# One table of moves in a convolution beside a gated unit: stores given to SyncE, late loads, fewer matmuls under the kernel's making, more in the spectra, output in halves

## The chip, the cores and the metric

The kernel runs on one core of one Trainium2 chip. The metric is the device time of one execution in microseconds (us). Before the change the median of 3 runs is 724.4 us (723.02 to 726.36). The profile comes from one further execution, whose own time is given below. TensorE (PE) multiplies matrices, VectorE (DVE) and ScalarE (ACT) work element by element, GpSimd (POOL) is a third and slower such engine, SyncE (SP) only issues transfers. ACT and POOL also issue transfers, in the one order in which all their instructions stand.

## The reference, cut to what matters

A row of the input is one of 2048 tokens with 448 channels; everything is float32.

```python
xn = _layernorm(x, axis=-1)
# A: a convolution over the tokens, its kernel K made from 256 complex modes per channel
P = jnp.exp((A * dt[:, None])[:, :, None] * pos[None, None, :])
K = 2.0 * jnp.einsum("dn,dnl->dl", C, P).real
y = jnp.fft.irfft(jnp.fft.rfft(u_t, L2) * jnp.fft.rfft(K, L2)[None], L2)[:, :, :L]
# B: a gated unit with 1792 inner columns
h = _sigmoid(xn @ w_gate) * (xn @ w_up)
out = x + (y + u * D_skip) + h @ w_down        # u_t is u = xn, tokens last
```

## The kernel before, in words

Two streams of work share the core, each written as a generator, and a planner takes turns between them. `conv` makes A, `glu` makes B and adds the residual x.

**conv.** First the modes are prepared. Then the convolution kernel K is made in 56 *chunks* of 8 channels (`kgen`). A chunk takes the angles' matmul (`tr`, L533) from a small tile `ph` that SP loads two pairs of chunks ahead (`phase_load`, L479 to 483), four ACT instructions for sines and cosines (`S`, L541 to 544), powers by POOL (`me`, `mf`, L511), three wide DVE products (`Et`, `Et`, `Ft`, L602 to 604), and 32 small matmuls (`ko`, L618; in the trace each is two, so 64). Every fourth chunk its result goes through a first stage of the transform (`kp`, `kq`, L559) and by ACT into DRAM (`sk_d`). Then comes `spectra`: 17 *steps*, one for each set of frequencies. A step loads the spectra's first stages of K (`skl`) and of the input (`sx`), transforms them (`there`, L891, 32 + 32 matmuls in the trace), multiplies them (DVE L897 to 905, POOL or DVE L907 and 908), makes halves (L912 and 913) and, two steps later, transforms them back (`back`, L926), writes them to DRAM (`v_d`) and reads them turned round (`vp`). `last` (L954 to 973) is the final transform from `vp`, once for each half h of the channels and each quarter q of the tokens: 32 matmuls in the trace, then DVE adds them to the accumulator. For h = 1 it then stores the rows of q to the output (L973).

**glu.** The tokens go in two halves of 1024, each as two tiles t of 512. For each of 14 pieces f of the inner columns and each t a `gate` does 11 matmuls for w_gate and 11 for w_up (`gu`, L709; "a gate half" below is 11 of them), then tanh by ACT (`th`, L717), a product by DVE (L720), and a split into high and low parts (`hh` by ACT, L725, `hl` by DVE, L727). After a group of 3 (once 2) pieces the down products run: per block b of 128 tokens 9 (or 6) matmuls (`po`, L812), which DVE adds to the accumulator `acc` (L817). The accumulators start as the residual x, loaded by `x_load` (L234). Half 0's are stored to `acc_d` (L832) and come back late in `spectra` as `ac`; half 1 takes the same two buffers, so its residual loads can start only when these stores have landed. These loads are issued by ACT.

**The crossing.** While the last group of half 0 runs, the second 1024 tokens come in, in four pairs (b = 8, 10, 12, 14): loaded, normalised, transposed (L207), and put through the first stage of the input's transform (`pair_first`, L685: 16 matmuls L273, four copies L693 by ACT into tiles `x1`, each stored by two transfers, L279, to `x1_d`; "x" and "x_d" in the trace). Two of the four copies go to a buffer that the next pair uses again (`wraw`), two to a pair of small buffers (`rd`).

**What sets the order.** The planner (L1135 to 1154) gives the next turn to the stream with the smaller share of its total done. A turn's share is the number that the generator yields: `WK / 3` three times a chunk, `WS / 2` twice a step, `2.5` a gate half, `0.6 * fc` a down block. The totals are in L1136. In `spectra` the turns simply alternate. `glu` stops after the first block of its last group (`yield None`, L803) and goes on when `conv` is written out; `last(1, q)` is written into its last blocks (L822 to 825). A scheduler then orders each engine's instructions by its own estimate of when each is ready; `tc.issue_after(x)` adds an order edge behind x for those instructions of the block that run on x's engine. Each engine runs its instructions strictly in the order that results.

```python
    total = [sum(Y0) + 11 * WP + 8 * WX + AHEAD + NCK * WK + HOLE + 19 * WS, 2 * (4 + NFT * 14.8) - HELD]
        i = min(live, key=lambda i: done[i] / total[i])
```

Of the kernel before, what the change touches and what calls it, by code (L numbers as in the profile page):

```python
# [20 lines left out]
D = 448  # L21
# [5 lines left out]
TWO_PI = 2.0 * math.pi  # L27
MAGIC = 1.5 * 2.0**23
NFT = F // 128
WK = 4.83  # L30
WS = 5
HOLE = 6
AHEAD = 34
WP = 5
WX = 2
HELD = 9
LASTS = 1
HP = 300
Y0 = (8, 1)
CP = D // 4  # L40
# [6 lines left out]
ORDER = [GROUPS, GROUPS[2:] + GROUPS[1::-1]]  # L47
# [79 lines left out]
def s4d_glu_kernel(ctx, tc, io):  # L127
    nc = tc.nc
# [556 lines left out]
    def pair_first(b, xns):  # L685

        x1 = pg.tile([128, 2, D], F32, name="x1", tag="wraw", bufs=1)
        pss = [psg.tile([128, 512], F32, name="gu", bufs=4) for _ in range(4)]
        for g in range(4):
            x_first_stage(pss[g][:, :D], xns, g)  # L690
        for g in range(4):
            to = x1[:, g] if g < 2 else pg.tile([128, D], F32, name="x1", tag="rd", bufs=RB)
            nc.scalar.copy(to, pss[g][:, :D])  # L693
            x1_store(row(b, g), to, nc.scalar)

    def gate(w, xs, to, between=None):
        wh, wl = w
# [32 lines left out]
    def glu():  # L730
        stores, later = [], []
        for half in range(2):
            if half == 1:
                for q in (2, 3):
                    accs.append(acc_tile())
                    x_load(accs[q], 4 * q, 4, [nc.scalar])
            for fs_ in ORDER[half]:
                fc, f0 = len(fs_), fs_[0]
                wts, ws, hs = [], [], [[], []]
# [12 lines left out]
                for n_, (f, t) in enumerate(order):  # L752
                    if t == 0:
                        wh = pg.tile([128, 2, 4, 128], F32R, name="wh", bufs=2)
                        if half == 0:
                            first = len(raws) == 2
                            raw, rd = raws.pop()
                            wl = w_low()
                            with hp(HP):
                                nc.scalar.copy(wh, raw)  # L760
                                if first:
                                    v.scalar_tensor_tensor(wl, raw, lim[:, 0, 0:1], wh, ALU.mult, ALU.subtract)
                                else:
                                    v.tensor_tensor(wl, raw, wh, ALU.subtract)
                            if not raws and f + 1 < NFT:
                                raws.append((w_load(f + 1), None))
                            stores.extend(kept((wh, wl), wt_d, f))
                        else:
                            wl = w_low()
                            for t_, d_ in kept((wh, wl), wt_d, f):  # L770
                                nc.sync.dma_start(t_, d_)
                        ws.append((wh, wl))
                    between = (lambda s_=mid[n_]: step(*s_)) if cross and mid[n_] else None
                    yield from gate(ws[f - f0], xq[2 * half + t], hs[t], between)
                    for t_, d_ in stores:
                        nc.sync.dma_start(d_, t_)
                    stores[:] = later
                    later.clear()
                    if t == 0:
                        dh = pg.tile([128, D], F32R, name="dh", bufs=FCH[0])  # L780
                        if half == 0:
                            rd = rd or rd_load(f)
                            dl = d_low()
                            with hp(HP), tc.issue_after((act if f == 1 else marks)[0].ins):
                                nc.scalar.copy(dh, rd)
                            nc.gpsimd.tensor_tensor(dl, rd, dh, ALU.subtract)
                            later.extend(kept((dh, dl), dt_d, f))
                        else:
                            dl = d_low()
                            for t_, d_ in kept((dh, dl), dt_d, f):  # L790
                                nc.sync.dma_start(t_, d_)
                        wts.append((dh, dl))
                    yield 2.5
                    for s_ in end[n_] if cross else ():
                        step(*s_)
                    if cross:
                        yield 2
                for t in range(2):
                    acc = accs[2 * half + t]
                    for b in range(4):  # L800
                        if final and (t, b) == (0, 1):

                            yield None  # L803
                        bs = slice(128 * b, 128 * b + 128)
                        end_ = final and (t, b) == (1, 3)
                        for h, ds in enumerate((slice(0, H), slice(H, D)) if end_ else (slice(0, D),)):
                            po = psg.tile([128, D], F32, name="po", tag="gu", bufs=4)
                            n = 0
                            with tc.issue_after(sp_mm[0].ins) if glu_on else nullcontext():
                                for (hh, hl), (dh, dl) in zip(hs[t], wts):  # L810
                                    for a_, w_ in ((hh, dh), (hh, dl), (hl, dh)):
                                        glu_mm[:] = [nc.tensor.matmul(  # L812
                                            po[:, ds], a_[:, bs], w_[:, ds], start=(n == 0), stop=(n == 3 * fc - 1)
                                        )]
                                        n += 1
                            with hp(HP):
                                v.scalar_tensor_tensor(  # L817
                                    acc[:, b, ds], po[:, ds], 0.5, acc[:, b, ds], ALU.mult, ALU.add
                                )
                            if final and t == 1 and b > 1:  # L820
                                out_end(acc[:, b : b + 1], 12 + b, ds)
                        if final and (t, b) == (1, LASTS):  # L822
                            sp_mm[:] = glu_mm
                            for q in range(4):
                                lasts[0](1, q)
                        if final and (t, b) == (1, 1):
                            out_end(acc[:, 0:2], 12, slice(0, D))
                        yield 0.6 * fc
                        if cross and (t, b) in downs:
                            step(*downs[t, b])  # L830
                    if cross:
                        nc.sync.dma_start(acc_d[:, 4 * t : 4 * t + 4], acc)  # L832

    def spectra(pf):
# [119 lines left out]
        def last(h, q):  # L954
# [15 lines left out]
                a = acc[:, p::2, ds]  # L970
                v.tensor_tensor(a, a, half(pb[q % 2][:, p, : 2 * H]), ALU.add)
            if h == 1 and q < 3:
                out_end(acc, 4 * q, slice(0, D), *([[nc.gpsimd]] if q == 0 else []))  # L973

        ac = acl[0]
        vts = [pf.tile([128, 4, H], F32, name="vt", bufs=2) for _ in range(2)]
# [57 lines left out]
        back(*made)  # L1034
        sp_mm[:] = glu_mm
        turned(*made[:2], 8, nc.gpsimd)
        back(*made_, (nc.sync, nc.scalar))
        turned(*made_[:2], 8)

# [141 lines left out]
```

## Time and profile before

| | |
|---|---|
| median of 3 runs | 724.4 us (723.02 to 726.36) |
| the profiled execution's own time | 727.67 us |
| its span, first to last instruction | 725.9 us |
| busy in the span: PE, DVE, ACT, POOL | 659.1, 575.6, 420.3, 351.6 us |
| first chunk's `ko` matmuls start, last chunk's | 146.2, 533.0 us |
| first step of `spectra`, last `back`'s first matmul | 547.7, 689.7 us |
| transfers | 125.76 MB, mean 173 GB/s |

In the answers below a row of the timeline reads: start in us, length in us, engine, line, operation, result<-operands, shapes, count, and in brackets the idle time of the engine before it and what ended that. A row of the chain of waits reads: start, length, what it was. A row of a table of stretches reads: from:to, length, then for PE, PEld (weight loads), DVE, ACT and POOL the busy us and (instructions), then the granted share of PE's clock, the mean busy share of the transfer engines, and GB/s. A matmul's row in a table of groups has the mean ns of one from issue to end; since matmuls overlap in the array, the time that a run of them takes is read from the chain.

### The profile page before, as it was taken

Reading aid. Unit: us, or ns where it says so; the run is one execution under the profiler, and the core shown is the slowest. Engines: PE = TensorE matmul, PEld = TensorE weight load, DVE = VectorE, ACT = ScalarE, POOL = GpSimd, SP = SyncE. Lnnn points to the kernel's source line nnn. Section 1 sums busy time; section 2 is a strip of 40 time slices with the busy share of each in tenths; the row PEclk is TensorE's granted clock in tenths of the full one; section 3 lists DMA queues with packets and bytes.
Section 4 is the critical chain, followed back from the end, with each engine's and each line's share of the span. In section 5 each row is a group of like instructions: output and inputs, shape, how many; then the busy total and the mean of one; then the engine's idle time right before and its main releaser. Section 6 shows DMA issues by size and latency. Waiting matters only on the chain.

```text
span 725.9 us, 20720 instructions
## 1 busy us (share of the span) xinstructions
PE 659.1 (91%) x8581; PEld 509.7 (70%) x8581; DVE 575.6 (79%) x779; ACT 420.3 (58%) x651; POOL 351.6 (48%) x395
## 2 busy tenths in 40 slices
PE   2798999999999899988979999999989999999784
PEld 1675788877778677655857887887776677777463
DVE  5689998699878798986548978897747989886823
ACT  3635455686678879996468768876822342332300
POOL 2111006785887879995335585686403224321101
PEclk9899999999899999999989999999989999999876
DMA  9977749645126454553962342433469787874456
GB/s 207 263 230 218 204 158 289 217 167 178 40 77 190 123 143 127 147 143 89 259 166 76 97 120 72 119 83 101 132 173 373 235 283 248 280 234 158 145 162 203
DMA packets 93630, 125.76 MB, mean 173 GB/s; under 512 B 12784, under 2 KB 79536, under 8 KB 93280
## 3 DMA queue, kind: packets, MB, share of 16 engines
q1 hardware_dynamic: 72000, 107.15, 46.9%
q10 hardware_dynamic: 20816, 14.91, 8.6%
q0 software_dynamic: 720, 2.36, 1.3%
q8 instruction: 68, 1.11, 0.6%
q14 instruction: 26, 0.21, 0.1%
HBM read 72.09 MB, written 52.30 MB: 171 GB/s over the span
## 4 chain that ended last, share of the span: by engine, by line
PE 49%; DVE 19%; DMA 10%; ACT 10%; issue 5%; POOL 3%; ACTq 1%; SPq 1%; DVEq 0%; POOLq 0%
PE gu L709 21%; PE po L812 13%; DVE Et L602 4%; DVE Ft L604 4%; DVE Et L603 3%; PE ko L618 3%; POOL me L511 2%; PE pk L891 2%; PE tr L533 2%; DMA x_d<-x 2%; PE px L891 2%; ACT S L544 2%; ACT S L541 2%; PE pk L926 1%; ACT S L542 1%
## 5 line engine op out<-in xcount | busy, mean ns | idle before, releaser
L511 POOL TENSOR_TENSOR me<-me,pm 128x32 f32<-128x32 f32 (+1 forms) x168 | 134.5, 801 | 97.3 <-DVE Et L603 85.1
L511 POOL TENSOR_TENSOR mf<-mf,pm 128x64 f32<-128x64 f32 (+1 forms) x112 | 121.0, 1080 | 5.8
L709 PE MATMUL gu<-xh,wh 128*128 128x512 f32 x336 | 103.5, 413 | 4.1 <-ACT xh L216 4.0
L603 DVE TENSOR_TENSOR Et<-me,S 128x1024 f32<-128x1024 f32 x56 | 79.2, 1414 | 23.0 <-ACT me L524 20.6
L709 PE MATMUL gu<-xh,wl 128*128 128x512 f32 x336 | 96.1, 392 | 0.0
L709 PE MATMUL gu<-xl,wh 128*128 128x512 f32 x336 | 95.9, 391 | 0.0
L812 PE MATMUL po<-dh,hh 128*128 128x448 f32 (+1 forms) x227 | 87.8, 387 | 2.9 <-DVE acc L817 1.4
L812 PE MATMUL po<-dh,hl 128*128 128x448 f32 (+1 forms) x227 | 84.9, 376 | 0.0
L725 ACT CAST hh<-gu 128x512 fp32r<-128x512 f32 x56 | 33.0, 590 | 89.3 <-DVE gu L720 82.5
L812 PE MATMUL po<-dl,hh 128*128 128x448 f32 (+1 forms) x227 | 84.6, 373 | 0.0
L604 DVE TENSOR_TENSOR Ft<-mf,S 128x1024 f32<-128x1024 f32 x56 | 78.3, 1399 | 7.5 <-POOL mf L511 3.9
L602 DVE TENSOR_TENSOR Et<-me,S 128x1024 f32<-128x1024 f32 x56 | 75.6, 1351 | 8.3 <-ACT S L544 7.9
L709 PEld LDWEIGHTS gu<-xh,wh 128*128 128x128 f32 x336 | 61.6, 193 | 26.6 <-issue 7.6
L618 PE MATMUL ko<-Et,Ft 128*32 128x64 f32 x3584 | 65.0, 224 | 12.4 <-DVE Ft L604 12.1
L618 PEld LDWEIGHTS ko<-Et,Ft 128*32 128x32 f32 x3584 | 54.8, 112 | 30.5 <-DVE Ft L604 16.8
L817 DVE SCALAR_TENSOR_TENSOR acc<-po,acc 128x448 f32<-128x448 f32 (+1 forms) x81 | 48.5, 609 | 33.0 <-PE po L812 33.0
L709 PEld LDWEIGHTS gu<-xh,wl 128*128 128x128 f32 x336 | 62.9, 188 | 14.6 <-DVE hl L727 0.7
L709 PEld LDWEIGHTS gu<-xl,wh 128*128 128x128 f32 x336 | 62.9, 188 | 14.2 <-issue 0.7
L541 ACT ACTIVATE S<-tr 128x1024 f32<-128x1024 f32 x56 | 57.9, 1034 | 25.7 <-PE tr L533 15.6
L907 POOL TENSOR_TENSOR yy<-yy 128x448 f32<-128x448 f32 (+1 forms) x16 | 23.5, 1471 | 92.7 <-DVE yy L904 92.7
L544 ACT ACTIVATE S<-S,hpi 128x1024 f32<-128x1024 f32 x56 | 65.9, 1176 | 0.1
L542 ACT ACTIVATE S<-tr 128x1024 f32<-128x1024 f32 x56 | 57.8, 1032 | 0.0
(204 smaller groups left out, 1268.1 us busy)
## 6 DMA issues: line engine op xcount, KB each, us to landing
wt_d<-wh SPq DMA_DIRECT2D x14, 512.0 KB
wt_d<-wl SPq DMA_DIRECT2D x14, 512.0 KB
sk_d<-sk ACTq DMA_DIRECT2D x28, 256.0 KB
wl<-wt_d SPq DMA_DIRECT2D x14, 512.0 KB
wh<-wt_d SPq DMA_DIRECT2D x14, 512.0 KB
sx<-x_d SPq DMA_DIRECT2D x16, 448.0 KB
skl<-sk_d SPq DMA_DIRECT2D x16, 448.0 KB
vp<-v_d SPq DMA_DIRECT2D x7, 896.0 KB
```

The source lines that it names most:

```text
L511: ins = nc.gpsimd.tensor_tensor(m[:, :, w + a : 2 * w : n], m[:, :, a:w:n], par(base + i).unsqueeze(2).to_broadcast([128, 4 * DC, w // n]) ...
L541: nc.scalar.activation(rows(cs), pv, AF.Abs)
L542: nc.scalar.activation(rows(S[:, 0:5:4]), pv, AF.Sin, scale=TWO_PI)
L544: sins[:] = [nc.scalar.activation(cs, cs, AF.Sin, scale=-TWO_PI, bias=hpi)]
L602: v.tensor_tensor(Et[:, :, :, 32:64], two(me[:, :, 32:64]), S[:, 1::-1], ALU.mult)
L603: v.tensor_tensor(Et[:, :, :, 0:32], two(me[:, :, 0:32]), S[:, 1:3, :, ::-1], ALU.mult)
L604: fts[:] = [v.tensor_tensor(Ft, two(mf), S[:, 3:5], ALU.mult)]
L618: nc.tensor.matmul(ko[32 * j : 32 * j + 32, sl], Ft[:, cc, DC * h + 4 * q + j], Et[:, cc, DC * h + 4 * q + j], start=(k == 0), stop=(k == ...
L709: glu_mm[:] = [nc.tensor.matmul(ps, a_, b_, start=(n == 0), stop=(n == len(mm) - 1))]
L725: nc.scalar.copy(hh, hf)
L812: glu_mm[:] = [nc.tensor.matmul(po[:, ds], a_[:, bs], w_[:, ds], start=(n == 0), stop=(n == 3 * fc - 1))]
L817: v.scalar_tensor_tensor(acc[:, b, ds], po[:, ds], 0.5, acc[:, b, ds], ALU.mult, ALU.add)
```

## The change

1. `WK` goes from 4.83 to 4.3. The planner counts less for a chunk, and so gives fewer `glu` turns to the 56 chunks and more to what lies before and behind them.
2. `pair_first` issues its stores by SP instead of ACT.
3. The residual loads of half 1 are written into its first group, behind the gates of turns n_ = 1 and n_ = 3 (gates of the second tile of tokens), inside `tc.issue_after(marks[1].ins)`; `marks[1]` is the gate's product on DVE (L720). They are still issued by ACT.
4. `last(0, q)` for q = 0 and 1 stores its half of the channels at once (SP); `last(1, q)` then stores only the other half for these q.
5. Before the last `back` one more turn is given to `glu`.
6. `LASTS` goes from 1 to 2: `last(1, q)` is written behind block (1, 2) instead of (1, 1), and blocks 0 to 2 leave in one store for each of 4 token groups.

```diff
-WK = 4.83
+WK = 4.3
-LASTS = 1
+LASTS = 2
...
-            x1_store(row(b, g), to, nc.scalar)
+            x1_store(row(b, g), to, nc.sync)
...
                     accs.append(acc_tile())
-                    x_load(accs[q], 4 * q, 4, [nc.scalar])
...
+                    if half == 1 and fs_ is ORDER[1][0] and n_ in (1, 3):
+                        q = 2 + n_ // 2
+                        with tc.issue_after(marks[1].ins):
+                            x_load(accs[q], 4 * q, 4, [nc.scalar])
                     yield 2.5
...
-                            if final and t == 1 and b > 1:
+                            if final and t == 1 and b > LASTS:
                                 out_end(acc[:, b : b + 1], 12 + b, ds)
                         if final and (t, b) == (1, LASTS):
                             sp_mm[:] = glu_mm
                             for q in range(4):
                                 lasts[0](1, q)
-                        if final and (t, b) == (1, 1):
-                            out_end(acc[:, 0:2], 12, slice(0, D))
+                            out_end(acc[:, : LASTS + 1], 12, slice(0, D))
...
             if h == 1 and q < 3:
-                out_end(acc, 4 * q, slice(0, D), *([[nc.gpsimd]] if q == 0 else []))
+                out_end(acc, 4 * q, ds if q < 2 else slice(0, D), *([[nc.gpsimd]] if q == 0 else []))
+            elif h == 0 and q < 2:
+                out_end(acc, 4 * q, ds, [nc.sync])
...
         turned(*made[:2], 8, nc.gpsimd)
+        yield WS / 2
+        sp_mm[:] = glu_mm
         back(*made_, (nc.sync, nc.scalar))
```

ScalarE at the start of half 1, before: `th_4272` and `hh_4275` belong to the first gate of half 1, `th_4367` to the second, `acc_4227` is the second residual buffer, `S`, `me` and `ks` belong to chunks.

```order
L717 ACTIVATE th_4272<-gu_4236 128x512
L544 ACTIVATE S0_1152<-S0_1152,hpi_72 128x2x512
L524 ACTIVATE me1_1146<-me1_1146 128x32x8
L524 ACTIVATE me1_1146<-me1_1146 128x32x16
L236 DMA acc_4227<-in_A_u_dram 32x1792 x2
L725 CAST hh_4275<-gu_4260 128x512
L236 DMA acc_4227<-in_A_u_dram 32x1792
L717 ACTIVATE th_4367<-gu_4318 128x512
```

The same place now, where the first gate has `th_4264` and `hh_4267`, and the buffer is `acc_4223`:

```order
L544 ACTIVATE S0_1183<-S0_1183,hpi_72 128x2x512
L524 ACTIVATE me1_1177<-me1_1177 128x32x8
L450 ACTIVATE pm0_1186<-pm0_1186,one_74 128x640
L524 ACTIVATE me1_1177<-me1_1177 128x32x16
L717 ACTIVATE th_4264<-gu_4228 128x512
L236 DMA acc_4223<-in_A_u_dram 32x1792 x2
L725 CAST hh_4267<-gu_4252 128x512
L236 DMA acc_4223<-in_A_u_dram 32x1792 x2
L717 ACTIVATE th_4359<-gu_4310 128x512
```

The first two loads of the second buffer still stand ahead of the first gate's `hh`; the edge to an instruction of DVE does not hold an instruction of ACT.

SyncE in the crossing before, between the weights of half 1 (`wh_4456`, `wl_4457`: its second piece) and the angles `ph` of coming chunks:

```order
L483 DMA ph1_1157<-phv_d_59 32x2x256
L771 DMA wh_4456<-wt_d_63 128x1024
L771 DMA wl_4457<-wt_d_63 128x1024
L483 DMA ph0_1156<-phu_d_58 8x2x256
L483 DMA ph0_1156<-phu_d_58 16x2x256
```

The same place now (`x1_3778`, `x1_3797` and `x1_3801` are the second pair's first-stage tiles, `wh_4452` and `wl_4453` the same weights):

```order
L483 DMA ph0_1187<-phv_d_59 32x2x256
L279 DMA x1_d_61<-x1_3778 64x2x224 x4
L279 DMA x1_d_61<-x1_3797 64x2x224 x2
L770 DMA wh_4452<-wt_d_63 128x1024
L279 DMA x1_d_61<-x1_3801 64x2x224 x2
L770 DMA wl_4453<-wt_d_63 128x1024
L483 DMA ph1_1188<-phu_d_58 8x2x256
```

The stores of L279 have joined this queue: the second weights and the angles behind them now stand behind the pair's stores, and the last of these behind one load of weights.

TensorE at the end of `spectra`, before: all matmuls of the last two steps and of the last four `back`s, with nothing of `glu` between.

```order
L891 MATMUL pk_6730<-skl_7998,tb_8000 32x224 x16
L891 MATMUL px_6731<-sx_7997,tb_8000 32x224 x16
L926 MATMUL pk_6730<-xx_8097,bk_6728 64x224 x8
L926 MATMUL px_6731<-xx_8097,bk_6728 64x224 x8
L891 MATMUL pk_6730<-skl_8108,tb_8110 32x224 x16
L891 MATMUL px_6731<-sx_8107,tb_8110 32x224 x16
L926 MATMUL pk_6730<-xx_8278,bk_6728 64x224 x8
L926 MATMUL px_6731<-xx_8278,bk_6728 64x224 x8
L926 MATMUL pk_6730<-xx_8448,bk_6728 64x224 x8
L926 MATMUL px_6731<-xx_8448,bk_6728 64x224 x8
```

Now, from the gate half behind the last `there` on (`xx_8200` is what the `back` of the step before the last but one takes, `xx_8375` the one after it):

```order
L709 MATMUL gu_8496<-xl_3862,wh_8385 128x512 x3
L928 MATMUL pk_6690<-xx_8200,bk_6688 64x224 x8
L928 MATMUL px_6691<-xx_8200,bk_6688 64x224 x8
L709 MATMUL gu_8530<-xh_3861,wh_8385 128x512 x3
L709 MATMUL gu_8530<-xr_3863,wh_8385 128x512
L709 MATMUL gu_8530<-xh_3861,wl_8386 128x512 x3
L709 MATMUL gu_8530<-xr_3863,wl_8386 128x512
L709 MATMUL gu_8530<-xl_3862,wh_8385 128x512 x3
L928 MATMUL pk_6690<-xx_8375,bk_6688 64x224 x7
L928 MATMUL px_6691<-xx_8375,bk_6688 64x224 x4
```

A gate half now stands between every two pieces of the last steps, and 9 down products stand ahead of the last `back`.

Counted over the whole order, `glu`'s 1913 matmuls lie so: ahead of the first chunk's `ko` 470 before and 485 now, ahead of the 20th and the 30th 850 and 986 before and 846 and 984 now, ahead of the 44th 1254 and 1267, ahead of the 56th 1466 and 1448, ahead of the first step of `spectra` 1507 and 1472.

## The prediction

> **What bounds the kernel now.** I first read the table of stretches, to see which engine is full where.
>
> ```profile
> 120.00:140.00 20.00, 20.00 (x98) 17.59 (x97) 10.72 (x22) 10.53 (x17) 11.84 (x24) 1.00 0.78 255
> 200.00:220.00 20.00, 18.76 (x317) 14.69 (x316) 16.36 (x17) 15.43 (x23) 15.62 (x18) 1.00 0.30 92
> 320.00:340.00 20.00, 16.24 (x224) 10.21 (x226) 16.28 (x21) 17.02 (x27) 16.46 (x19) 0.91 0.50 134
> 340.00:360.00 20.00, 20.00 (x244) 15.15 (x241) 8.68 (x13) 9.06 (x16) 6.23 (x11) 1.00 0.77 193
> 360.00:380.00 20.00, 15.21 (x294) 12.19 (x293) 10.32 (x14) 10.61 (x17) 5.70 (x11) 0.83 0.70 206
> 460.00:480.00 20.00, 20.00 (x325) 16.48 (x324) 18.86 (x19) 15.72 (x23) 15.85 (x15) 1.00 0.27 88
> 600.00:620.00 20.00, 20.00 (x318) 15.20 (x302) 18.82 (x31) 6.12 (x12) 7.51 (x6) 1.00 0.65 216
> 680.00:700.00 20.00, 17.08 (x194) 12.76 (x179) 11.65 (x17) 4.57 (x9) 3.63 (x3) 0.74 0.54 149
> ```
>
> TensorE is full ahead of the chunks (120 to 140), nearly full in the later chunks (460 to 480) and in the spectra (600 to 620), where DVE stands at 94% too. In the early chunks (200 to 220) four engines share the bound. Two places are loose: the crossing, 320 to 380, and the end, from 680. There the clock also falls. So time can be had in those two, and elsewhere only by moving matmuls of `glu` from a full place into a loose one.
>
> Next, the crossing on ACT, with the group row of the stores and the chunk that TensorE waits for:
>
> ```profile
> L279 ACTq DMA_DIRECT2D x_d<-x x32: 582/617/1983, 301.1 to 352.3; - x32
> 344.67 4.41 ACTq L279 DMA_DIRECT2D x_d<-x  x4
> 349.12 0.53 ACT L693 COPY x<-gu 128x448 f32<-128x448 f32 x1 [3.98 <-DMA x_d<-x]
> 353.00 0.59 ACT L631 COPY ks<-ko 128x512 f32<-128x512 f32 x1 [2.91 <-DMA x_d<-x]
> 357.74 8.16 DMA acc_d<-acc
> 367.01 0.59 ACT L725 CAST hh<-gu 128x512 fp32r<-128x512 f32 x1 [6.64 <-issue]
> 369.50 1.93 PE L618 MATMUL ko<-Et,Ft 128*32 128x64 f32 x64 [4.79 <-DVE Ft L604]
> 351.52 1.15 DVE L817 SCALAR_TENSOR_TENSOR acc<-po,acc 128x448 f32<-128x448 f32 x2
> ```
>
> ACT stands 3.98 and 2.91 us while it issues four stores each time, and 6.64 us in front of the second residual load, which waits for the store of the accumulator (issued at 357.74, landed at 365.90). TensorE goes on with `glu` meanwhile and feels this once, 4.79 us.
>
> The end, by the chain of waits:
>
> ```profile
> 660.91 0.76 PE px L891 x32
> 661.67 2.76 PE gu L709 x11
> 665.48 2.73 PE gu L709 x11
> 668.20 0.94 PE pk L962 x32
> 672.81 2.02 PE po L812 x9
> 674.83 1.00 PE pk L891 x32
> 692.96 6.28 DMA v_d<-vt
> 699.26 6.15 DMA vp<-v_d
> 711.94 4.03 PE po L812 x27
> ```
>
> Between the gate halves of 661.67 and 665.48 lies one `back`, 664.43 to 665.48. `glu` has stopped at 674.83; the last steps run bare until the last spectrum goes out at 692.96 and is back at 705.41. Then come four `last`s at half clock, 27 down products, and the output. TensorE's own gaps and the stretches here:
>
> ```profile
> 683.41 1.08 PE L926 MATMUL pk<-xx,bk 32*64 32x224 f32 x16 [1.92 <-DVE kk L898]
> 705.55 1.78 PE L962 MATMUL pk<-vp,wf 64*32 64x224 f32 x32 [3.15 <-DMA vp<-v_d]
> 685.00:690.00 5.00, 4.00 (x49) 2.35 (x42) 4.86 (x7) 1.67 (x4) 0.00 (x0) 0.50 0.36 89
> 705.00:710.00 5.00, 4.45 (x96) 3.05 (x96) 1.97 (x4) 0.00 (x0) 1.03 (x3) 0.50 0.02 3
> 710.00:715.00 5.00, 5.00 (x68) 4.07 (x53) 3.27 (x7) 0.00 (x0) 0.95 (x2) 0.85 0.97 251
> 715.00:720.00 5.00, 0.96 (x9) 0.77 (x7) 0.77 (x2) 0.00 (x0) 0.00 (x0) 0.83 0.98 313
> 720.00:725.90 5.90, 0.00 (x0) 0.00 (x0) 0.00 (x0) 0.00 (x0) 0.00 (x0) 0.50 0.47 147
> ```
>
> From 710 the transfer engines are full: the whole output, 251 x 5 + 313 x 5 + 147 x 5.9 = 3.7 MB, leaves in the last 16 us.
>
> **The change part by part.** The rates: a gate half of 11 takes 2.73 us, 0.248 each; 9 down products 2.02, 0.224 each. The sum is made on the span, 725.9 us; the profiled execution took 727.67, and the median is 724.4, so I subtract from the median.
>
> *A. Stores by SP, later loads.* 32 issues of 0.617 us, 19.7 us, leave ACT. They were not all on the path: felt by ACT are 3.98 + 2.91 us, and TensorE was full from 340 to 360 all the same. The loads do not move: in ACT's order the first two of the second buffer still stand between the first gate's `th` and `hh`, since the edge is to an instruction of DVE. So ACT still waits for the accumulator's store. That store needs DVE's last add, which ended at 352.67, yet it went out at 357.74, behind loads in SP's queue that reuse the pair's buffers and so wait until ACT has issued the pair's stores and they have landed. Issued by SP right behind the copies, they are done some 4 to 5 us sooner, and the accumulator's store with them. What the path feels is the 4.79 us of TensorE and its clock: 0.83 of 20 us is 6.8 us at half speed, 3.4 us lost; together 8.2. Bounds: 0 (ACT comes early to the same wait) and -12 (all of this, and the 3.8 us that TensorE is idle from 320 to 340). I take **-5**. What waits on SP behind the stores are angles and weights; the angles are loaded some three chunks of 7 us ahead of their use, and 19.7 us of issue fit into SP's idle time, which in this stretch is mostly waiting for tiles to be free:
>
> ```profile
> SPq L483 <- PE tr L533: 31.6, 5, 9.5
> ```
>
> One sentence of the Trainium skill speaks against A: "DMA: Bandwidth & Descriptors", Issuing engines are not separate DMA queues, says that issuing from several engines saves only the sequencer's time, "usually small relative to the DMA itself". Here that time is the row of 617 ns; by the page's word A would be 0.
>
> *B. Before the first chunk* stand 15 more matmuls, 3.7 us on a full TensorE. The chunks up to the 12th have 15 fewer, but there TensorE is not the only bound. Bounds 0 and +4; I take **+2**.
>
> *C. From the 45th to the 56th chunk* stand 18 fewer, 4.2 us. TensorE is full there, DVE at 94%: between 0 and -4.2, I take **-2.5**.
>
> *D. The spectra and the bare end.* From 674.83 to the issue at 692.96 are 18.1 us, the last 1.1 of them ACT's copies, which stay. Now four gate halves and nine down products lie in this stretch, 12.9 us; with its own matmuls at full clock (two `there` of 1.00 + 0.76, four `back` of 1.05, 7.7 us) and the copies that is 21.7, so it grows by 3.6. The matmuls come out of C and of the first three steps. From the last `kq` to the fourth step there were 30 down products and 55 of gates, 20.4 us; now 48 down products, 10.8 us: 9.6 fewer. There the cover becomes thin:
>
> ```profile
> L905 DVE TENSOR_TENSOR xx<-kk,xx 128x896 f32<-128x896 f32 x16 | 23.2, 1448 | 0.2
> L904 DVE TENSOR_TENSOR yy<-kk,xx 128x896 f32<-128x896 f32 x16 | 17.3, 1083 | 0.1
> L897 DVE TENSOR_TENSOR kk<-pk,oo 128x448 f32<-128x448 f32 x16 | 10.0, 623 | 15.8 <-ACT oo L895 15.6
> L912 DVE TENSOR_TENSOR xx<-yy 128x448 f32<-128x448 f32 x16 | 9.8, 615 | 0.0
> 536.57 6.92 SPq L860 DMA_DIRECT2D skl<-sk_d  x2
> 537.35 7.88 PE po L812 x30
> 550.60 0.96 PE pk L891 x16
> ```
>
> A step costs DVE 4 x 0.62 + 1.08 + 1.45 + 2 x 0.62 = 6.2 us and two adds of 0.6; TensorE, with two times 6 down products, only 1.76 + 1.05 + 2.7 = 5.5. So in up to three steps DVE decides, at about 2 us each. The second step needs `skl`, issued only at 543.5 when the chunk's last store has landed; TensorE reached it at 550.6 and now comes some 5 us sooner, to a wait of up to 2 us. I take 4 us of new waits, half of the 8 that these rows allow. Sum: 3.6 - 9.6 + 4 = **-2**; bounds -6 (no new wait) and +3 (all 8, and one more us for the steps after).
>
> *E. After the last `vp`.* Of the output 2 x 4 x 128 rows of 896 bytes, 0.92 MB, leave earlier, in the spectra, where the transfer engines have room (0.65). At 232 GB/s, the mean of these 15.9 us, this is 4.0 us, at the 313 of the full stretch 2.9. The rest in these quarters goes in pieces of 896 bytes, not of 7168, whose price no row shows. And 54 down products (12.1 us) instead of 45 cover the 12.5 us of store and load, so TensorE is idle for 1.5 us where it was for 3.15; if the clock then stays up, four `last`s take 4 x 0.94 = 3.8 us instead of 6.4, and the stores start a little over 1 us earlier. Bounds -2 and -6, I take **-4**. By the Trainium skill ("TensorE: Matmul & The Clock Gate", Part 1) the clock falls after an idle window of some 3.4 us, and would stay up here, for -5; but the trace has it at 0.50 from 685 on behind shorter gaps (1.92 us the longest), so the rule does not settle it.
>
> Sum: -5 + 2 - 2.5 - 2 - 4 = -11.5, and 724.4 - 11.5 = 712.9, **713 us**.
>
> **The rivals.** *1. A is nothing.* The load still stands in ACT's way, and TensorE was full during ACT's stalls; for it speaks 20.00 of 20 us at 340, against it 4.79 us and the fallen clock at 360. 713 + 5 = 718. The sentence of the Trainium skill on issuing engines would give the same. *2. All of it lands*: A -9, D -5, E -6, B +1.5, C -3: 724.4 - 21.5 = 703. For it speaks that idle time on TensorE also costs its clock, so a gap closed pays twice. *3. SP becomes the wait.* It runs its queue in order; a store in it waits for ACT's copy, and behind it stand `ph` and the weights. It decides once SP is later than the three chunks, some 21 us, by which `ph` is ahead; 4 pairs x 8 issues x 0.6 us = 19.7 us would then lie on the path, less the 6.5 of the other terms: 724.4 + 13 = 737. Against it speaks the 31.6 us that SP stands idle in front of `ph`. *4. Moving changes nothing*: the chunks with fewer matmuls are bound by DVE (C 0, B +4), the thinly covered steps as well (D +2), A is -4, E -4: 722.4, no change.
>
> **How the numbers follow.** Forecast 0.43, rival 1 0.20, rival 2 0.13, rival 3 0.10, rival 4 0.14. Less than 0.5% (3.6 us) can't be told from no change, so faster means under 720.8: 0.43 + 0.20 + 0.13 = 0.76; within 0.14; slower, over 728, 0.10. The range 704 to 725 leaves out rival 3 and the better half of rival 2.
>
> **What would show it.** ACT has no first-stage stores between the copies of the crossing, the wait in front of `hh` is still there but under 5 us, and the clock stays at 1.00 around it (A). The first chunk starts about 149 instead of 146.2 (B). TensorE is idle for short times in the first three steps, and not from there to the last `back` (D). From the landing of the last `vp` to the end are some 16.5 us instead of 20.5 (E). I am wrong if SP's stores wait longer than ACT's did, if the first steps of the spectra stretch by more than the end shrinks, or if the transfers in halves of rows are so slow that the last 16 us stay.

## The result, and the profile after

The changed kernel takes 711.05 us (median of 4 runs, 710.86 to 711.65), the kernel before in the same job 723.71 (722.07 to 726.36): ratio 0.9837, 95% interval 0.9805 to 0.9869. The forecast was 713.0 with a range of 704 to 725. The profiled execution took 710.88 us, its span 709.1.

The sum came out, but not by its terms. Table of stretches, cut where the first, 20th, 32nd and 56th chunk's `ko` matmuls start; the kernel before, then the changed one:

```profile
0.00:146.20 146.20, 126.22 (x590) 98.28 (x591) 119.36 (x231) 77.14 (x126) 41.47 (x62) 0.96 0.78 224
146.20:283.10 136.90, 127.36 (x1905) 103.64 (x1904) 123.06 (x130) 107.31 (x155) 106.21 (x111) 0.98 0.43 129
283.10:376.80 93.70, 81.64 (x1242) 56.90 (x1241) 67.28 (x83) 66.93 (x109) 60.44 (x69) 0.95 0.58 160
376.80:533.00 156.20, 150.63 (x2436) 123.28 (x2435) 131.27 (x136) 119.52 (x171) 98.55 (x118) 1.00 0.37 107
533.00:725.90 192.90, 173.28 (x2417) 127.63 (x2417) 134.66 (x200) 49.38 (x94) 44.95 (x38) 0.92 0.69 226
```

```profile
0.00:149.30 149.30, 130.43 (x601) 101.74 (x601) 120.75 (x234) 78.20 (x128) 44.20 (x64) 0.98 0.77 220
149.30:275.90 126.60, 119.35 (x1880) 97.11 (x1879) 117.25 (x124) 101.58 (x146) 108.74 (x106) 1.00 0.46 137
275.90:376.60 100.70, 91.33 (x1261) 62.72 (x1260) 74.67 (x85) 73.62 (x120) 60.33 (x72) 0.90 0.56 156
376.60:522.50 145.90, 145.08 (x2408) 118.04 (x2407) 130.01 (x131) 116.19 (x166) 113.73 (x118) 1.00 0.35 100
522.50:709.10 186.60, 169.16 (x2436) 124.45 (x2435) 133.47 (x205) 49.55 (x95) 53.24 (x38) 0.97 0.75 242
```

Beside these lengths stand `glu`'s matmuls in each stretch, counted in the trace, at the prediction's 0.248 us each:

| stretch | before, us (matmuls) | after, us (matmuls) | difference | matmuls moved | rest |
|---|---|---|---|---|---|
| to the first chunk | 146.2 (470) | 149.3 (485) | +3.1 | +3.7 | -0.6 |
| 1st to 20th chunk | 136.9 (380) | 126.6 (361) | -10.3 | -4.7 | -5.6 |
| 20th to 32nd (holds the crossing) | 93.7 (159) | 100.7 (173) | +7.0 | +3.5 | +3.5 |
| 32nd to 56th | 156.2 (457) | 145.9 (429) | -10.3 | -6.9 | -3.4 |
| 56th to the end | 192.9 (447) | 186.6 (465) | -6.3 | +4.5 | -10.8 |
| span | 725.9 | 709.1 | -16.8 | +0.1 | -16.9 |

The matmuls only change place; what is won is the last column. The profiled execution of before lies 4 us above its median (727.67 us against 723.71), so some 4 of these 16.8 us are scatter; in which stretch they lie is not known. The two stretches of chunks win 20.6 us, 9.0 of them beyond the matmuls that moved, where the prediction had -2.5 for the last chunks and nothing for the others. The crossing loses 7.0 us, 3.5 beyond its matmuls, where the prediction had a gain of 5.

**In the chunks** gaps go. One example, with the slow clock around it: stretches with the sixth chunk, before (two rows) and after (two rows), and between them the row of TensorE's timeline that ends the gap of before:

```profile
180.00:187.00 7.00, 4.32 (x39) 2.78 (x35) 6.28 (x6) 6.91 (x11) 4.87 (x5) 0.67 0.17 59
187.00:195.00 8.00, 8.00 (x133) 7.06 (x129) 6.44 (x8) 4.08 (x7) 6.61 (x9) 0.86 0.35 74
```

```profile
182.78 1.22 PE L533 MATMUL tr<-sel,ph 128*128 128x512 f32 x2 [2.68 <-ACT S L543]
```

```profile
181.00:185.00 4.00, 4.00 (x107) 3.03 (x99) 4.00 (x6) 3.91 (x7) 2.49 (x4) 1.00 0.00 0
185.00:190.00 5.00, 5.00 (x116) 3.98 (x104) 5.00 (x5) 4.53 (x8) 4.79 (x4) 1.00 0.15 33
```

Before, 5 matmuls of `glu` lie between the 5th and the 6th chunk and 24 before the 7th; TensorE stood 2.68 us, and its clock is 0.67 around that gap and 0.86 behind it. Now they are 7 and 12, and nothing stands there. Not every gap goes: from the 1st to the 20th chunk TensorE's idle time (length less busy time in the table) falls from 9.5 to 7.3 us, and gaps of 1.89, 2.61 and 1.92 us now stand at other chunks. From the 32nd to the 56th chunk it falls from 5.6 to 0.8 us, at full clock in both kernels; 2.66 us of that stood in front of the last chunk, which had no matmul of `glu` between it and the one before and now has 14.

**In the crossing** a row of the changed kernel's waits (us in all, times, longest), then its timeline of SP and ACT, and its stretches:

```profile
SPq L279 <- ACT x L693: 16.9, 7, 4.7
```

```profile
346.58 7.99 SPq L279 DMA_DIRECT2D x_d<-x  x8
357.65 0.38 SPq L834 DMA_DIRECT2D acc_d<-acc  x1
366.23 0.59 ACT L725 CAST hh<-gu 128x512 fp32r<-128x512 f32 x1 [7.32 <-DMA acc_d<-acc]
323.00:340.00 17.00, 15.98 (x170) 8.31 (x170) 9.64 (x15) 9.22 (x16) 5.11 (x9) 0.70 0.35 88
360.00:370.00 10.00, 9.13 (x186) 7.17 (x187) 5.23 (x8) 3.35 (x5) 3.90 (x5) 1.00 0.68 208
```

ACT no longer issues first-stage stores. But the accumulator's store goes out at 357.65, as before (357.74). SP's eight stores, which wait for ACT's copies, and a few loads stand in front of it; yet the last add that it needs also comes later, at 356.05 instead of 352.67, so it waits 1.6 us behind that add, where before it waited 5.1. `hh` waits 7.32 us instead of 6.64; in the three other profiles with this order of the crossing it waits 4.77, 5.89 and 7.64. TensorE hardly feels that (9.13 of 10 us), and the clock is at 1.00 there. The clock now falls earlier, to 0.70 over the 17 us from 323 on, behind two gaps:

```profile
323.03 0.73 PE L533 MATMUL tr<-sel,ph 128*128 128x512 f32 x2 [2.03 <-ACT S L543]
324.75 2.08 PE L273 MATMUL gu<-xt,wx 32*64 32x448 f32 x8 [0.99 <-DVE xl L214]
```

TensorE's busy time between the 20th and the 32nd chunk grows by 9.7 us: 3.5 are the matmuls that moved there, and some 5, estimated from a mean clock of 0.90 instead of 0.95, are the clock. Its idle time falls, from 12.1 to 9.4 us.

**The end**: TensorE's timeline at the first steps of the spectra, the chain of waits, and two tables of stretches.

```profile
531.37 0.99 PE L893 MATMUL pk<-skl,tb 64*32 64x224 f32 x32 [0.51 <-DMA skl<-sk_d]
534.27 0.57 PE L893 MATMUL pk<-skl,t 64*32 64x224 f32 x4 [1.16 <-DVE kk L900]
536.98 1.07 PE L893 MATMUL pk<-skl,t 64*32 64x224 f32 x10 [2.14 <-DMA skl<-sk_d]
```

```profile
681.16 4.99 DMA v_d<-vt
686.17 5.77 DMA vp<-v_d
692.07 1.13 PE pk L964 x32
696.58 2.21 PE po L815 x18
```

```profile
680.00:690.00 10.00, 10.00 (x63) 8.99 (x52) 2.68 (x5) 0.98 (x2) 0.52 (x1) 1.00 0.79 229
690.00:700.00 10.00, 7.85 (x154) 5.92 (x153) 6.22 (x12) 0.00 (x0) 2.22 (x4) 1.00 0.38 90
```

TensorE is full and at full clock during the round trip of the last spectrum; the four `last`s take 4.5 us instead of 6.4. From the landing of the last `vp` to the end are 709.1 - 691.94 = 17.2 us, before 20.5.

The largest entry of the last column, -10.8 behind the 56th chunk, is in great part the clock. Two stretches of before, and one after:

```profile
534.00:540.80 6.80, 6.12 (x87) 5.44 (x76) 0.62 (x1) 1.71 (x3) 0.54 (x1) 0.50 0.47 108
684.20:694.40 10.20, 9.20 (x93) 6.12 (x88) 5.71 (x9) 3.10 (x6) 0.01 (x1) 0.50 0.50 125
```

```profile
541.00:701.00 160.00, 155.15 (x2183) 113.92 (x2181) 123.59 (x191) 45.18 (x87) 49.54 (x35) 1.00 0.75 243
```

Before, TensorE worked 15.3 us in these two stretches at half clock, and again during the `last`s, where 32 matmuls took 1.78 us (705.55 before) and now take 1.02 at full clock (694.50 after). By that ratio, an estimate, the two stretches lost some 6 us; now the clock is at half only for some 3 us ahead of 541, and after 701, where TensorE has no work left.

### The profile page after: what moved, and what is told of

It is laid out like the page before. It is cut to its first block, busy times and chain, and to the rows that moved or that the text cites. A ratio compares the mean times of both kernels' runs of the same rounds, so it can differ in the third digit from the quotient of the medians.

```text
span 709.1 us, 20743 instructions
## 1 busy us (share of the span) xinstructions
PE 655.4 (92%) x8581; PEld 504.1 (71%) x8581; DVE 576.2 (81%) x779; ACT 419.2 (59%) x651; POOL 380.2 (54%) x395
## 5 line engine op out<-in xcount | busy, mean ns | idle before, releaser
L511 POOL TENSOR_TENSOR me<-me,pm 128x32 f32<-128x32 f32 (+1 forms) x168 | 155.0, 922 | 72.4 <-DVE Et L603 59.1
L511 POOL TENSOR_TENSOR mf<-mf,pm 128x64 f32<-128x64 f32 (+1 forms) x112 | 116.3, 1039 | 6.5
L604 DVE TENSOR_TENSOR Ft<-mf,S 128x1024 f32<-128x1024 f32 x56 | 80.8, 1444 | 5.0 <-PE ko L618 2.3
L909 POOL TENSOR_TENSOR yy<-yy 128x448 f32<-128x448 f32 (+1 forms) x16 | 31.6, 1975 | 91.0 <-DVE yy L906 91.0
L618 PEld LDWEIGHTS ko<-Et,Ft 128*32 128x32 f32 x3584 | 54.4, 111 | 25.3 <-issue 10.8
```

What stands on the lines that cost most here:

```text
L511: ins = nc.gpsimd.tensor_tensor(m[:, :, w + a : 2 * w : n], m[:, :, a:w:n], par(base + i).unsqueeze(2).to_broadcast([128, 4 * DC, w // n]) ...
L604: fts[:] = [v.tensor_tensor(Ft, two(mf), S[:, 3:5], ALU.mult)]
L618: nc.tensor.matmul(ko[32 * j : 32 * j + 32, sl], Ft[:, cc, DC * h + 4 * q + j], Et[:, cc, DC * h + 4 * q + j], start=(k == 0), stop=(k == ...
```

## The experiments

Kernels of one job share the runs of the kernel before, whose medians were 723.24 to 724.24 us. The changed kernel was run again too.

**The changed kernel again** (no edit):

> The changed kernel once more, no edit, on the chip of this call. If its runs scatter as those of the kernels with one edit undone (up to 10 us between runs of one kernel), some of the differences so far are smaller than they look: 709 to 720. If it is steady: 710.5 to 712, and the differences stand.

708.3 us (706.91 to 712.82), 0.9807 (0.976 to 0.9854). With the first four runs: 706.9 to 712.8, so a difference of 3 us between medians of different jobs says nothing. The kernels with WK, the stores or the end undone and the one with the other edge of the loads ran in one job.

**WK.** Set back in the changed kernel:

```diff
-WK = 4.3
+WK = 4.83
```

> The changed kernel (711.05 us) with WK back at 4.83; the five other edits stay. Theory 1, from the traces of before and after: the chunks' gain is WK's. First chunk's ko to the 20th take 126.6 us instead of 136.9, the 32nd to the 56th 145.9 instead of 156.2, at 3.1 us for the later first chunk: so 711 + 10.3 + 10.3 - 3.1 = about 728, and about 721 if the crossing too goes back to its old length (93.7 instead of 100.7 us). Theory 2, the prediction's terms B (+2) and C (-2.5) and the 9.6 us of gates in the first steps: WK is worth under 4 us, 711 to 715. Theory 3: what the chunks gained comes with the other order of stores and loads, not with WK: 711, and the 126.6 us stay.

718.4 us, 0.9935 (0.991 to 0.996). The new number as the only change to the kernel before:

> The kernel before (724.4 us) with WK = 4.3 as the one edit. Theory 1 (the edits add up): 724.4 - 7.4 = 717. Theory 2 (WK makes the stretches without first-stage stores shorter, and the crossing longer as long as ScalarE issues these stores): 20th to 32nd chunk some 106 us, as with the stores undone in the changed kernel; by stages 149.3 + 126.5 + 106.5 + 145.7 + (192.9 - 3.0) = 718 of span, 719.7. Theory 3 (alone it is worth nothing): 723 to 725.

723.91 us, 0.9981 (0.9958 to 1.0005). Stretches of the first, then of the second kernel, 1st to 20th, 20th to 32nd, 32nd to 56th chunk:

```profile
143.30:280.20 136.90, 127.19 (x1905) 103.50 (x1904) 124.07 (x130) 107.19 (x155) 107.11 (x110) 0.98 0.43 129
280.20:372.30 92.10, 81.24 (x1254) 57.59 (x1255) 69.20 (x83) 68.60 (x114) 60.79 (x70) 0.96 0.60 168
372.30:527.00 154.70, 148.59 (x2430) 121.52 (x2432) 131.98 (x136) 116.53 (x167) 99.78 (x118) 1.00 0.36 106
```

```profile
150.20:279.20 129.00, 122.75 (x1884) 99.38 (x1885) 118.48 (x125) 103.93 (x149) 111.35 (x109) 0.97 0.46 136
279.20:384.00 104.80, 87.38 (x1259) 61.92 (x1258) 74.47 (x86) 73.88 (x118) 57.28 (x73) 0.92 0.56 149
384.00:530.00 146.00, 145.49 (x2410) 118.23 (x2410) 128.02 (x130) 115.41 (x163) 109.72 (x114) 1.00 0.34 100
```

The chunks' gain is WK's, with the stores on either engine: 129.0 and 146.0 us against 136.9 and 154.7. But WK alone gives it back: the crossing takes 104.8 us instead of 93.7, and the first chunk starts later (150.2). So theory 1 of the first text holds in its stretches (its 721 was 3 us too high, and the start scatters by as much); theory 2 of the second holds for the crossing, not for the time: alone WK is worth nothing that can be told, which is its theory 3.

**The stores.** Issued by ScalarE again in the changed kernel; by SyncE in the kernel before, as its only change; and by GpSimd in the changed kernel:

```diff
-            x1_store(row(b, g), to, nc.sync)
+            x1_store(row(b, g), to, nc.scalar)
```

> The changed kernel (711.05 us) with the stores of the first stage issued by ScalarE again; the rest stays. Theory 1 (term A as predicted, -5): 716, and the 20th to the 32nd chunk take longer than 100.7 us. Theory 2 (SyncE is the worse issuer here, as the crossing of 100.7 us against 93.7 of before suggests): the crossing goes back to some 94 us, 704 to 706. Theory 3 (the issuer is off the path, the longer crossing is WK's): 711, within 1.5 us.

717.95 us, 0.9926 (0.9893 to 0.9959): theory 1 by time and by the crossing.

> The kernel before (724.4 us) with the first-stage stores issued by SyncE as the one edit. Theory 1 (term A, -5, and the 6.9 us that undoing it in the changed kernel cost): 717 to 719, and the 20th to the 32nd chunk 88 to 89 instead of 93.6 us. Theory 2 (with WK = 4.83 the stores of ScalarE lie where TensorE is full, as the 92.1 us of the kernel with WK undone suggest): 722.5 to 724.

723.78 us, 1.0001 (0.9976 to 1.0025): theory 2.

> The changed kernel (711.05 us, 708.3 in its second job) with the stores of the first stage issued by GpSimd, neither by ScalarE (717.95) nor by SyncE. Theory 1 (what pays is that ScalarE does its copies and casts without issues between them; GpSimd is busy 60.6 us of the 101 from 276 to 377, so it has room): 708 to 712, and the 20th to the 32nd chunk 98 to 102 us. Theory 2 (an issue delays whatever stands behind it in a busy engine's queue; on GpSimd these are the powers me and mf, from which the chunks' products are made): the 20th to the 32nd chunk 104 to 110 us, 715 to 720.

712.03 us, 0.9825 (0.9802 to 0.9849): theory 1 at its upper end, in the crossing a little past it. The stretch from the 20th to the 32nd chunk of the three, in this order:

```profile
275.80:382.30 106.50, 93.61 (x1263) 66.19 (x1263) 74.01 (x86) 75.42 (x121) 57.73 (x76) 0.86 0.54 149
```

```profile
279.90:375.40 95.50, 83.21 (x1250) 59.29 (x1249) 70.67 (x85) 69.94 (x115) 62.79 (x72) 0.93 0.58 162
```

```profile
277.40:380.50 103.10, 92.98 (x1260) 64.19 (x1259) 77.94 (x86) 75.03 (x121) 78.00 (x107) 0.85 0.53 153
```

With WK at 4.3 the crossing takes 104.8 and 106.5 us where ScalarE issues, and 98.1 to 101.8 where SyncE does (five profiles with the turns of the crossing as changed: 100.7, 101.8, 98.4, 98.1, 100.2); with 4.83 it takes 93.7 where ScalarE issues, 92.1 and 95.5 where SyncE does. So the issuer matters only in the order that WK = 4.3 makes: in the changed kernel undoing either costs some 7 us, and on the kernel before neither pays alone. The kernel before with just these two was not run, so that none of the other edits is needed for it is not shown; nor were the late loads, LASTS or the extra turn undone one by one. What pays is that ScalarE is rid of the issues, for GpSimd as issuer gives nearly the same time, though it too has to wait for the copies; its crossing of 103.1 us, in one profile, lies between those of the other two. In the changed kernel with ScalarE's stores, TensorE's first stage waits 3.85 us for the DVE half of the transposing split, which stands behind two wide products of a chunk; in the kernel with GpSimd's stores, the second row, nearly as long:

```profile
328.09 0.97 PE L273 MATMUL gu<-xt,wx 32*64 32x448 f32 x4 [3.85 <-DVE xl L214]
329.44 2.36 PE L273 MATMUL gu<-xt,wx 32*64 32x448 f32 x8 [3.41 <-DVE xl L214]
```

The longest such wait in the changed kernel is 0.99 us. But GpSimd's kernel has the wait and not the time, so this row alone does not explain the 6 to 7 us. By what path ScalarE's issues cost them stays open, and which of the 32 makes the difference was not separated.

**The residual loads.** The edge put on an instruction of the engine that issues them:

```diff
-                        with tc.issue_after(marks[1].ins):
+                        with tc.issue_after(marks[0].ins):
```

> The changed kernel (711.05 us), the edge of the late residual loads put behind the gate's tanh, an instruction of ScalarE, the engine that issues them, instead of the product on VectorE. Now the first hh of half 1 stands ahead of them. Theory 1: ScalarE's wait of 7.32 us in front of hh is gone, and the path feels 3 to 6 us of it: 705 to 708. Theory 2: TensorE is full there all the same (9.13 us of 10 from 360 to 370), the wait cost nothing: 710 to 711.

710.76 us (706.81 to 712.37), 0.9822 (0.9784 to 0.986): theory 2. The loads now stand behind the first `hh`, which waits for DVE alone:

```profile
358.90 0.59 ACT L725 CAST hh<-gu 128x512 fp32r<-128x512 f32 x1 [3.45 <-DVE gu L720]
361.22 0.33 ACTq L236 DMA_DIRECT2D acc<-in_A_u_dram  x1
```

The wait for the store, 7.32 us, is gone and the time stays: it cost nothing.

**The place of the 27th chunk.** In the changed kernel it comes 17.7 us after the 26th, behind 12 matmuls of `glu` and a whole pair. A turn of the crossing that counts a little more puts it earlier; in a second kernel the edge above is added; in a third also a credit that takes the difference back after the crossing:

```diff
-                        yield 2
+                        yield 2.25
...
                         nc.sync.dma_start(acc_d[:, 4 * t : 4 * t + 4], acc)
+                        if t == 1:
+                            yield -1.5
```

> The changed kernel (711.05 us), where a turn of the crossing counts 2.25 instead of 2 in the planner. The 27th chunk's ko matmuls then stand behind 910 of glu's matmuls, 54 transposing ones and 48 of the first stage, as with WK at 4.83, instead of behind 916, 56 and 56; up to the 26th chunk the order is the same. Theory 1: the longer crossing of the changed kernel (26th to 28th chunk 32.4 us, before 26.0) comes from this place; it falls to some 26 us, and the time to 704 to 706. Theory 2: TensorE falls to half clock there after its two waits whatever stands behind them; 711, and 31 to 33 us from the 26th to the 28th chunk.

721.11 us, 0.994 (0.9911 to 0.997).

> Both the turn of the crossing at 2.25 and the edge of the late residual loads on ScalarE's tanh, in the changed kernel. Theory 1 (two separate losses, the place of the 27th chunk 5 to 7 us, the wait in front of hh 2 us): 701 to 704. Theory 2 (with the place mended the wait is hidden, or the other way round): 704 to 706. Theory 3 (neither matters): 710 to 711.

718.91 us, 0.991 (0.9879 to 0.9941).

> The kernel of both edits (crossing turns at 2.25, edge on ScalarE's tanh: 718.9 us), which also takes the 6 x 0.25 = 1.5 shares back after the crossing's last block. Then 1448 matmuls of glu lie ahead of the 56th chunk again, as in the changed kernel, instead of 1437. Theory 1 (those two kernels lost their time where glu is handed over: 11 matmuls more behind the chunks, and TensorE busy 15 to 16.5 us of 20 from 540 to 560 instead of 18.80): from the 56th chunk to the end some 187 us instead of 193.9, the crossing stays at 94: 705 to 708. Theory 2 (the loss comes from the crossing's new order itself, or the chunks behind it): 716 to 720.

712.6 us, 0.9846 (0.9811 to 0.988). The 26th to the 28th chunk took between 24 and 25 us in all three instead of 32.4, as wanted, and nothing was won: none of the first two texts' theories had a slower kernel. Stretches from the 20th chunk to the 32nd, to the 56th and to the end, of the second, then of the third kernel:

```profile
275.50:369.50 94.00, 85.84 (x1248) 59.96 (x1247) 75.06 (x85) 72.07 (x117) 61.33 (x76) 0.91 0.55 150
369.50:522.60 153.10, 147.66 (x2413) 120.08 (x2413) 129.80 (x131) 118.00 (x168) 99.33 (x114) 0.99 0.36 104
522.60:716.50 193.90, 174.99 (x2446) 127.66 (x2446) 136.32 (x205) 49.79 (x95) 45.94 (x38) 0.95 0.73 235
```

```profile
276.90:371.70 94.80, 87.42 (x1252) 60.58 (x1254) 73.55 (x85) 71.97 (x117) 60.56 (x76) 0.87 0.54 148
371.70:523.40 151.70, 147.59 (x2420) 120.70 (x2419) 128.58 (x131) 117.74 (x168) 107.65 (x114) 1.00 0.38 107
523.40:712.20 188.80, 170.29 (x2436) 125.31 (x2435) 136.50 (x205) 49.75 (x95) 45.67 (x38) 0.96 0.73 240
```

The stretch to the 32nd chunk then holds 161 matmuls of `glu` instead of 173, so 3 of its 4 to 7 us are only moved: in the second kernel behind the 56th chunk, in the third into the chunks ahead of it (441 instead of 429). These chunks, from the 32nd to the 56th, take 153.1 and 151.7 us instead of 145.9, and TensorE is idle in them for 5.4 and 4.1 us instead of 0.8. In the second kernel 11 matmuls were left over after the 56th chunk; the credit puts them back, and the end takes 188.8 us instead of 193.9. Eleven matmuls are 2.7 us; the rest was lost at the start of the spectra, where TensorE is busy 16.45 of 20 us at a clock of 0.76 (540 to 560) in the second kernel, 18.41 in the third. Theory 1 of the third text holds for the end and fails for the time, since the gain in the crossing is lost in the chunks.

**The end.** The last three edits of the diff undone together (output in halves, the turn before the last `back`, LASTS), then the output in halves alone:

```diff
-                out_end(acc, 4 * q, ds if q < 2 else slice(0, D), *([[nc.gpsimd]] if q == 0 else []))
-            elif h == 0 and q < 2:
-                out_end(acc, 4 * q, ds, [nc.sync])
+                out_end(acc, 4 * q, slice(0, D), *([[nc.gpsimd]] if q == 0 else []))
```

> The changed kernel (711.05 us) without the output in halves, without the turn before the last back, and with LASTS = 1. Theory 1 (term E, -4, and the covered round trip): from the landing of the last vp to the end 20 us again instead of 17.2, the clock at 0.5 there, 715 to 716. Theory 2 (the end is not what sets the time; what the gates fill there is only moved from the chunks): 711 to 712.

716.63 us, 0.9914 (0.9885 to 0.9943).

> The changed kernel (711.05 us) without the output in halves alone; LASTS = 2 and the extra turn stay. Theory 1 (most of the 5.6 us that the three edits of the end were worth are the 0.92 MB that leave earlier, 2.9 to 4.0 us): 714 to 715. Theory 2 (most is TensorE's cover of the round trip and its clock): 711.5 to 712.5.

715.93 us, 0.9885 (0.985 to 0.992). Both lie a little above their theory 1 and far from theory 2. Beside the changed kernel's second run, in the same job, the halves are worth 7.6 us, beside its first 4.9; in the traces the stretch behind the 56th chunk is 189.4 us long without them and 186.6 with them, and the rest is scatter ahead of it. The stretches after TensorE's last work in the kernel without halves, then in the changed one:

```profile
705.00:710.00 5.00, 0.00 (x0) 0.00 (x0) 0.00 (x0) 0.00 (x0) 0.00 (x0) 0.50 0.95 332
710.00:714.40 4.40, 0.00 (x0) 0.00 (x0) 0.00 (x0) 0.00 (x0) 0.00 (x0) 0.50 0.27 88
```

```profile
700.00:705.00 5.00, 0.00 (x0) 0.00 (x0) 0.00 (x0) 0.00 (x0) 0.00 (x0) 0.61 0.93 322
705.00:709.10 4.10, 0.00 (x0) 0.00 (x0) 0.00 (x0) 0.00 (x0) 0.00 (x0) 0.50 0.25 71
```

TensorE's last down products end at 700.87 and 698.79: 13.5 and 10.3 us before the end. The 3.2 us are the 0.92 MB at some 300 GB/s. LASTS and the extra turn add 0.7 by the medians, less than can be told.

## Why the prediction was right in its sum and wrong in some of its terms

*The sum.* Three things made it, each worth some 5 to 7 us when it is undone: the output in halves, WK, and the stores, the last two only together. -11.5 had been put together in part from other pieces, so that it came so close to the -12.7 measured is in part luck.

*A (-5): the size came out, the steps to it failed.* Undoing the stores costs 6.9 us, but not by the second load. "So ACT still waits" held, but the wait was 7.32 us instead of falling under 5; and it was free, as the kernel with the edge on ScalarE shows. The 4.79 us of TensorE and the clock at 0.83 were there in the trace of before; the step that fails is to take them for what the stores cost, by way of an accumulator's store that goes out "some 4 to 5 us sooner". In the kernel before with the stores alone moved to SyncE this store still waits 5.9 us behind its last add (349.39 to 355.25; before 5.1), `hh` waits 6.75 us, and TensorE stands nearly as long:

```profile
365.45 1.93 PE L618 MATMUL ko<-Et,Ft 128*32 128x64 f32 x64 [4.26 <-DVE Ft L604]
```

So with WK at 4.83, the order from which the 4.79 us were read, the stores' issuer is worth nothing (723.78 against 724.05). The term's bound of 0, "ACT comes early to the same wait", was the right reading of that order. What A is worth arises only in the other order, which the prediction did not look at, so that its size came out is luck. The loads did not move, as said.

The sentence of the Trainium skill, "DMA: Bandwidth & Descriptors", Issuing engines are not separate DMA queues, says that more issuing engines save only the sequencer's time, usually little. That it is the issuing engine's time which counts agrees: SyncE and GpSimd do alike. That it is little does not hold in every order: 0 us in one, 6 to 7 in the other, of 32 issues at 0.61 us.

*B (+2) and C (-2.5): the start as forecast, the chunks far off.* The first chunk starts at 149.3, said was 149. But the failing step is "there TensorE is not the only bound", from which fewer matmuls were worth nothing up to the 12th chunk and at most their own time behind it. The stretch from the 1st to the 20th chunk became 10.3 us shorter for 4.7 of matmuls, that from the 32nd to the 56th 10.3 for 6.9, since TensorE's idle time falls with WK. Between the 1st and the 20th chunk it is 9.5 to 9.8 us in the three profiles with 4.83 and 5.7 to 7.4 in the eleven with 4.3; between the 32nd and the 56th 5.4 to 6.1, and 0.4 to 0.8 in the eight with 4.3 and the turns of the crossing as changed. The prediction counted matmuls per stage and did not look at how they lie chunk by chunk. They do not lie much more evenly now (0 to 33 a chunk in these two stretches before, 2 to 35 after), but no chunk there is left without any; that this is what closes the gaps is argued from the trace, not tested. It also counted at the 30th chunk (986 and 984) and so did not see that 14 more lie between the 20th and the 32nd.

*D (-2): the waits as said, the gain not seen.* The new waits in the first three steps are 0.51 + 1.16 + 2.14 = 3.8 us, 4 were taken, and behind them TensorE waits once for 1.07 us and once for 0.51 up to the last `back`. From the last `kq` to the last spectrum's store are 155.4 us, before 155.6: -0.2, inside the bounds of -6 and +3.

*E (-4): as said, by another split.* 17.2 us from the landing to the end, 16.5 were forecast, and the round trip took 10.8 us instead of 12.5. By the medians the halves are most of it (4.9 of the 5.6 us of the three edits), in the traces 2.8 of 4.6 us behind the 56th chunk; the price of pieces of 896 bytes, unknown then, does not show, for the last stretch still moves 322 GB/s. The clock stayed at 1.00 through a gap of 0.46 us. The rule of the Trainium skill, "TensorE: Matmul & The Clock Gate", Part 1, by which it falls after an idle window of some 3.4 us, is against other rows of this case: 0.70 behind gaps of 2.03 and 0.99 us, 0.67 around one of 2.68.

*The rivals.* Rival 4, "moving changes nothing", is true of WK alone and of the stores alone, and false of the two. Rival 3 fell: SP waits 16.9 us for ACT's copies, and the kernel is no slower for it. Rival 1 is right for the order of before. Rival 2 fell by the time, though its reason, that a gap closed also brings back the clock, is seen in the chunk shown above and behind the 56th chunk.

## What to carry to other kernels

A stall read in the trace of before prices an edit only as long as the order around it stays; where another edit changes the order, price the two together, or run each alone and both. When a planner's number moves work, count it per chunk, not per stage: what is won is not the moved work but the gaps that go, and a gap on TensorE can cost a slow clock as well. A gain seen in one stretch is one only if the work in that stretch is the same, so put a count of matmuls beside each length.

## What was not expected of the hardware

TensorE's granted clock can fall around gaps of 2 to 3 us (2.68 us, and 0.67 of the clock around it; 2.03 and 0.99 us, then 0.70 over 17 us). Not every such gap does it: in the changed kernel a gap of 2.61 us ends at 241.2 us and the clock is at 1.00 from 236 to 250; in the second run of the same kernel the same gap, 2.60 us, is followed by 0.51 from 242.5 to 245.9. And the first chunk's start scatters by 3 to 4 us between kernels with the same order ahead of it: 146.2, 143.3 and 142.7 us with 470 matmuls of `glu` ahead of it, 146.9 to 150.8 with 485. What moves it was not looked into.
